# Three edits at the start of a fused attention and two-MLP kernel: coarse exponentials from PSUM, six products of zeros, and a new order of all steps

## The chip, the cores and the metric

The kernel runs on one core of one Trainium2 chip. The metric is the device time of one execution in microseconds. The core has five engines that this text calls TensorE (PE in the rows, PEld for its weight loads), VectorE (DVE), ScalarE (ACT), GpSimd (POOL) and SyncE (SP, which here issues all DMAs). Each works through its own queue in program order and waits on semaphores for the others.

## The reference

Attention of two kinds over q, k, v of 4 batches, 8 heads, 576 positions and 64 columns is added up, and two MLPs follow.

```python
q_d = q.reshape(B, H, Sd, 4, D).mean(axis=3)     # k_d, v_d likewise, Sd = 144
out_up = np.repeat(sm_attn(q_d, k_d, v_d), 4, axis=2)          # coarse
mask = np.abs(pos[:, None] - pos[None, :]) < 4
scores = np.where(mask, scale * q @ k.T, -1e9)                 # local
out = out_up + softmax(scores) @ v
x = out.transpose(0, 2, 1, 3).reshape(2304, 512)
h = x @ w_in;  x = (h * np.cos(h)) @ w_out                     # 512 -> 2048 -> 512
out = ((x @ w_a) * (x @ w_b)) @ w_out2                         # 512 -> 1536 -> 512
```

Both softmaxes subtract the maximum of a row, and divide by the sum plus 1e-9.

## The kernel before

The tokens are cut into eight units of 288 (two to a batch). A unit's attention is done in four head pairs `hp`, two of which form a `pr`. Every step of attention and of the first MLP is a key in the string `ORDER`, and the loop at lines 972 to 983 emits the steps in that order, so that each engine's queue is the order of the keys that fall to it. A key is a name, the unit and the pair, and after @ the engine (a ScalarE, d VectorE, p GpSimd) where there is a choice. The last third of the run, the second MLP, is emitted by loops and not by `ORDER`.

The steps of one unit:

- `sm` sums q and k in fours (line 373 on VectorE, three instructions at 375 to 377 on GpSimd); `lp` and `dp` are the local and the coarse scores on TensorE (398, 422). `vp` (344, unit 0 only) sums v in fours on TensorE.
- `lm` adds the mask and takes the maximum (405, 410), `lu` subtracts it (415), `le` is the exponential (442), `ln` and `lz` sum and divide (458 to 464).
- `dx` takes the coarse maximum (428). `da` writes maximum minus score into the tile `smd` (436 on ScalarE, 438 on VectorE), and `de` is its exponential with a scale of -1/128 and a row sum (449; each row sum shows as an extra ACTIVATION_READ_ACCUMULATOR). From unit 2 on (`DM` is 2) one `de` serves both pairs of a unit. `dn` and `dz` turn the sums into factors and apply them (476, 486).
- `lt`, `dt` transpose (493, 505), `lc`, `dc`, `vq`, `up` copy out of PSUM (290, 292), `at` multiplies with v (518 coarse, 525 local), `cb` adds the two parts (538), and `xh`, `xl` split the result into a rounded part and a rest (290 or 292, 560).

The first MLP: `w3.0` to `w3.4` convert the fourth block of weights in five stages (266, 269 on ScalarE, 271 on VectorE, a copy, a subtraction at 580). `h` (group g, part c) is three products of the first layer, `c` six stages of x cos x (656 to 668: ScalarE, VectorE, ScalarE, VectorE, a copy, a subtraction), `b` three products of the second layer. The stages c.4 and c.5, w.3 and w.4, and `xh` and `xl` may run on any engine that `ORDER` names. Exponential and sine need different tables of ScalarE, and a change of table is an ACT_TABLE_LOAD. Keys that begin with L are loads (`L0` the first ones: k and q of a pair, v for two pairs as `v` and `V`, weights as `w`), those with `p` prepare the second MLP's weights.

Scores of unit 0 go to several PSUM tags; from unit 1 on all of a unit's attention shares the one buffer of the tag `att`, so each use waits for the last reader of the one before. The tag `h` has two buffers.

Of the kernel before, what the change touches and what calls it, by code (L numbers as in the profile page):

```python
# [47 lines left out]
C = {'FS': 8, 'DM': 2, 'LAG': 3, 'NGS': 3, 'NGH': 4, 'NLAST': 9, 'CP': 24, 'SD0': 2, 'RA': 7, 'SA': 6, 'SD': 3, 'LG': 6, 'NXF': 3, 'LI': 2.5, 'LO': 2.5, 'L0': ['k0', 'k1', 'v0', 'V0', 'w0', 'k2', 'w1', 'k3', 'v1', 'V1', 'w2', 'w3', 'w4', 'w5', 'w6', 'w7']}  # L48
# [7 lines left out]
sm1.1@d Lc10 vq0.2@a ln0.1 lz0.1@d vq0.3@a Lc8 h0.0 w6.2@d h1.0 w9.1@a dz0.2@p dt0.1 dc0.1@a w3.0@a h1.1 Lq2.0 lt0.1 lc0.10@a lc0.11@a at0.1 w5.2@d  # L56
h2.0 h2.1 w6.3@d w10.1@a w9.2@d w3.1@a up0.1@d cb0.2 xh0.2@a cb0.3 w6.4@p w3.2@d h0.1 L0w7 sm1.0@d xh0.3@a xl0.3@d w8.1@a lp1.0 xl0.2@p h2.2 h1.2
w3.3@d h0.2 h0.3 w8.0@a w4.3@a w8.2@d w7.1@a lm1.0 c0.0@a w3.4@p Lc12 w4.4@p c0.1@d Lc15 Lk2.1 h1.3 c1.0@a c1.1@d Lc26 w7.0@a w7.2@d w7.3@d Lq1.2
w5.3@d h2.3 c2.0@a h3.0 h3.1 c0.2@a Lc13 h3.2 h3.3 c3.0@a dp1.0 c1.2@a dx1.0 w7.4@p Lq1.3 lu1.0@p c0.3@d da1.00@d c1.3@d lu1.1@d h5.0 h5.1 h5.2
da1.01@d sm1.2@d lp1.1 sm1.3@d w5.4@p c2.1@d Lk2.0 h4.0 Lc16 w12.0@a c0.4@d c1.4@d c1.5@p Lc27 w10.0@a w12.1@a w8.3@d Lc11 h4.1 lm1.1 h4.2 c0.5@p b0.1  # L60
w9.3@a h5.3 w10.2@d lu1.2@p le1.0 ln1.0 lz1.0@p de1.0 dn1.0 b0.0 Lc30 c2.2@a c3.1@d c2.3@d h4.3 dp1.1 dx1.1 da1.10@d w11.1@a c4.0@a Lc29 da1.11@d b1.0
lu1.3@p b0.3 b1.3 w8.4@d b1.1 dz1.0@p lt1.0 lc1.00@d lc1.01@d c3.2@a c3.3@d w9.4@d c2.4@a w13.0@a c2.5@p b2.0 b2.1 le1.1 dz1.1@p c3.4@d c3.5@p w15.1@a
dt1.0 ln1.1 dc1.0@a w10.3@a sm2.0@d b2.3 b0.2 w10.4@p b1.2 at1.0 b3.0 up1.0@d Lq2.1 c4.1@d w11.0@a cb1.1 c5.0@a b2.2 de1.1 b3.1 cb1.0 b3.3 dn1.1
lz1.1@p lt1.1 b3.2 c4.2@a Lw2.0 w11.2@d Lc18 lc1.11@a lc1.10@a Lc14 w11.3@a dz1.3@p sm2.1@d lp2.0 xh1.1@a c4.3@d c5.1@d lm2.0 vs2.0@p w15.0@a Lc24
xl1.1@d xh1.0@a w11.4@p h6.0 h6.1 Lc22 c4.4@a Lq2.2 dz1.2@p c5.2@a c5.3@d h6.2 Lc20 w14.1@a h6.3 c6.0@a w13.1@a lu2.1@p dt1.1 Lc19 dc1.1@d c5.4@a
c6.1@d w12.2@d c4.5@d h7.0 w14.0@a w12.3@a h7.1 at1.1 up1.1@a w14.2@d cb1.2 cb1.3 Lc25 c6.2@a c6.3@d h7.2 h7.3 c7.0@a xh1.2@a xh1.3@a xl1.0@p dp2.0
Lc21 w12.4@p b4.3 w13.2@d Lw2.1 Lk2.3 h8.0 w19.0@a b4.0 c7.1@d c7.2@a dx2.0 Lq2.3 c7.3@d w13.3@a h8.1 w20.1@a w20.0@a xl1.2@p h8.2 da2.00@d xl1.3@p
w15.2@d da2.01@d h9.0 h9.1 Lk2.2 h9.2 w27.0@a h9.3 vs2.1@p c6.4@a Lq3.0 lp2.1 c5.5@p h8.3 b4.1 w25.0@a w13.4@d b5.3 b5.1 sm2.3@d c6.5@p lm2.1 w14.3@a
w14.4@p Lc23 b4.2 b5.2 Lc17 b5.0 b6.0 lu2.0@p lu2.2@p c8.0@a c8.1@d w16.0@a Lc28 sm2.2@d c9.0@a c9.1@d b6.3 w24.0@a dp2.1 c8.2@a c8.3@d c7.4@d b6.1
lu2.3@p h10.0 w15.3@a w15.4@p dx2.1 da2.10@d h10.1 h10.2 c9.2@a le2.0 b6.2 Lv2 Lq3.2 da2.11@d h10.3 de2 c10.0@a c9.3@d c7.5@p b7.2 b7.0 ln2.0 Lw2.2  # L70
vs2.2@p h11.0 b7.1 le2.1 Lq3.1 lz2.0@p h11.1 c10.1@d c10.2@a dn2 h11.2 h11.3 c11.0@a c8.4@a c10.3@d b7.3 e7.0@d sm3.1@p e7.3@d lt2.0 dz2.0@p lc2.01@a
# [1199 lines left out]
```

## Time and profile before

| | us |
|---|---|
| median of three runs | 896.27 (894.94 to 896.31) |
| the profiled execution | 895.03 |
| its span from the first to the last instruction | 893.2 |
| TensorE busy | 872.7 (98%) |
| VectorE busy | 658.0 (74%) |
| ScalarE busy | 551.5 (62%) |
| GpSimd busy | 497.0 (56%) |

The profile's busy time of TensorE counts each product with its modelled end, so products overlap in it and a busy engine need not be at its peak. Idle time of an engine matters only where the engine that ends last waits for it. All times below are counted from the start of the span.

### The profile page before, as it was taken

To read this page: it belongs to the slowest core of one execution; us is meant where nothing else is said; L and a number is where in the kernel's file an instruction comes from. 1 tells how busy PE (TensorE), PEld (TensorE's weight loads), DVE (VectorE), ACT (ScalarE), POOL (GpSimd) and SP (SyncE) were. 2 spreads that over 40 slices of the span, in tenths; PEclk is the share of its full clock that TensorE was granted. 3 is DMA by queue.
4 is the path that set the end of the run, shared out by engine and by line. 5 is a ranking of instruction groups with operands and counts; after the bars stand their busy time and mean duration, and the time that the engine had idled before them with its cause. 6 is when DMAs were issued, how large, how long until landed. Compare 5 with 4: busy or idle time off the path is not lost.

```text
span 893.2 us, 17805 instructions
## 1 busy us (share of the span) xinstructions
PE 872.7 (98%) x6444; PEld 815.2 (91%) x6444; DVE 658.0 (74%) x1229; ACT 551.5 (62%) x1126; POOL 497.0 (56%) x656
## 2 busy tenths in 40 slices
...
GB/s 356 327 309 142 121 120 80 129 154 112 221 214 176 163 142 159 89 43 126 270 310 115 95 180 213 289 241 273 343 93 71 183 206 260 341 73 96 232 139 54
DMA packets 96935, 162.10 MB, mean 181 GB/s; under 512 B 6608, under 2 KB 64464, under 8 KB 96848
## 3 DMA queue, kind: packets, MB, share of 16 engines
...
## 4 chain that ended last, share of the span: by engine, by line
PE 93%; DMA 2%; DVE 2%; ACT 1%; POOL 1%; issue 1%; SPq 0%; POOLq 0%; ACTq 0%
PE z L587 15%; PE z L588 15%; PE z L589 15%; PE acc L587 8%; PE h L587 8%; PE acc L588 7%; PE acc L589 7%; PE h L588 7%; PE h L589 7%; PE att L398 1%; DMA raw<-in_w_in_dram 1%; PE att L422 1%; PE att L525 1%; DMA kq<-in_kq_dram 1%; PE att L493 1%; PE att L518 1%
## 5 line engine op out<-in xcount | busy, mean ns | idle before, releaser
L1006 POOL TENSOR_TENSOR sb<-w,sb 128x256 fp32r<-128x256 f32 x154 | 125.2, 825 | 121.0 <-ACT sb L1004 120.2
L1004 ACT ACTIVATE sb<-w 128x256 fp32r<-128x256 f32 x252 | 97.8, 415 | 51.6 <-PE z L589 43.4
L587 PE MATMUL h<-xbig,w 128*128 128x480 f32 (+3 forms) x352 | 128.1, 364 | 1.5 <-DVE gbig L662 1.5
L587 PE MATMUL acc<-tbig,w 128*128 128x480 f32 (+3 forms) x352 | 127.4, 362 | 0.5 <-DVE gbig L662 0.5
L588 PE MATMUL acc<-tbig,w 128*128 128x480 f32 (+3 forms) x352 | 124.5, 354 | 1.2 <-POOL tbig L668 1.2
L588 PE MATMUL h<-xbig,w 128*128 128x480 f32 (+3 forms) x352 | 124.2, 353 | 0.7 <-POOL xbig L560 0.7
L589 PE MATMUL acc<-tbig,w 128*128 128x480 f32 (+3 forms) x352 | 124.4, 353 | 0.1
L589 PE MATMUL h<-xbig,w 128*128 128x480 f32 (+3 forms) x352 | 124.0, 352 | 0.0
L668 POOL TENSOR_TENSOR tbig<-gbig,tbig 128x288 fp32r<-128x288 f32 (+3 forms) x47 | 51.7, 1102 | 96.5 <-ACT tbig L290 45.4
L656 ACT ACTIVATE gbig<-h,turn 128x480 int32<-128x480 f32 (+3 forms) x88 | 53.3, 607 | 69.7 <-PE h L589 63.9
L587 PE MATMUL z<-xbig,sb 128*128 128x384 f32 x288 | 96.2, 334 | 0.0
L589 PE MATMUL z<-xbig,sb 128*128 128x384 f32 x288 | 96.2, 334 | 0.0
L588 PE MATMUL z<-xbig,sb 128*128 128x384 f32 x288 | 96.2, 334 | 0.0
L658 DVE SCALAR_TENSOR_TENSOR gbig<-gbig,h 128x480 f32<-128x480 int32 (+3 forms) x88 | 51.3, 585 | 57.0 <-ACT gbig L656 56.5
L1006 DVE TENSOR_TENSOR sb<-w,sb 128x256 fp32r<-128x256 f32 x98 | 60.0, 614 | 21.8 <-ACT sb L1004 21.8
L587 PEld LDWEIGHTS h<-xbig,w 128*128 128x128 f32 x352 | 66.2, 188 | 10.5 <-DVE gbig L662 2.1
L587 PEld LDWEIGHTS acc<-tbig,w 128*128 128x128 f32 x352 | 66.2, 188 | 8.8 <-issue 1.5
L588 PEld LDWEIGHTS acc<-tbig,w 128*128 128x128 f32 x352 | 66.2, 188 | 7.8 <-POOL tbig L668 1.9
L588 PEld LDWEIGHTS h<-xbig,w 128*128 128x128 f32 x352 | 66.3, 188 | 6.8 <-POOL xbig L560 1.2
L589 PEld LDWEIGHTS acc<-tbig,w 128*128 128x128 f32 x352 | 66.1, 188 | 6.5 <-POOL w L580 0.3
L589 PEld LDWEIGHTS h<-xbig,w 128*128 128x128 f32 x352 | 66.2, 188 | 6.2
L660 ACT ACTIVATE gbig<-gbig,turn 128x480 f32<-128x480 f32 (+3 forms) x88 | 56.5, 644 | 22.9 <-DVE gbig L658 22.3
...
## 6 DMA issues: line engine op xcount, KB each, us to landing
...
```

Source lines behind the costliest of these rows:

```text
L398: pe.matmul(p[i][o, W * w:W * w + W], qt[u, 2 * pr + i][r, off:off + W], kt[u, 2 * pr + i][r, off:off + W], start=True, stop=True)
L422: pe.matmul(p[a][:QD, SD * i:SD * i + SD], qd[u, 2 * pr + i][r, :], kd[u // 2, 2 * pr + i][r, :], start=True, stop=True)
L493: pe.transpose(p[part][:, 128 * i:128 * i + 128], pt[u, pr][:, s], ident)
L587: i = pe.matmul(ps_out, lh, rh, start=start, stop=False, skip_group_check=more)
L588: pe.matmul(ps_out, lh, rl, start=False, stop=False, skip_group_check=more)
L589: pe.matmul(ps_out, ll, rh, start=False, stop=stop, skip_group_check=more)
L656: act.activation(out=gs[g].bitcast(I32), in_=hps[g], func=AF.Identity, scale=1.0 / (2.0 * math.pi), bias=turn[:, 0:1])
L658: dve.scalar_tensor_tensor(out=gs[g], in0=gs[g].bitcast(I32), scalar=-2.0 * math.pi, in1=hps[g], op0=ALU.mult, op1=ALU.add)
L660: act.activation(out=gs[g], in_=gs[g], func=AF.Sin, bias=turn[:, 1:2])
L668: eng.tensor_tensor(out=gl[g], in0=gs.pop(g), in1=gh[g].bitcast(F32), op=ALU.subtract)
L1004: act.activation(out=t[:, 0], in_=blk, func=AF.Copy)
L1006: (dve if nst[0] % (C["SD"] if G else C["SD0"]) == 0 else pool).tensor_tensor(out=t[:, 1], in0=blk, in1=t[:, 0].bitcast(F32), op=ALU.subtract)
```

## The change

- `down_exp` (units 0 and 1) reads the coarse scores from PSUM, and takes the maximum times -1/128 as a bias. That product is one more small instruction in `down_max`. The eight `down_neg` of these units are gone.
- `down_sums` is cut in two: `sm` sums q, a new step `sk` sums k for both halves of a batch.
- The array with the first q and k has q ahead of k now, and each of its four loads is two: `L0k` brings q and the first half of k, `L0K` the rest.
- Six new steps `fw` each multiply 128x128 zeros with 128x256 zeros into a PSUM tile that nobody reads; VectorE clears 384 columns of `gbig` for them. They stand ahead of the first scores.
- `ORDER` is new from end to end: other sequence and, for many steps, another engine. The keys are the same but for those above. Copies (`xh`, w.3, c.4) on GpSimd, of which the old order has none, occur 47 times.

The diff, with the first lines of both orders:

```diff
-C = {'FS': 8, ...
+C = {'NW': 6, 'FS': 8, ...
 ORDER = """
-L0k1 L0k0 lp0.0 sm0.0@p sm0.1@d dp0.0 L0w1 w1.0@a w1.1@a lm0.0 L0v0 L0k3 w1.2@d lu0.1@d L0V0 vp0.0 lu0.0@d dx0.0 L0w2 w1.3@d le0.0 ln0.0 lz0.0@d lt0.0
-da0.01@a da0.00@a de0.0 L0k2 L0w0 w2.1@a w2.0@a Lq1.1 L0w5 vq0.0@a vq0.1@a sm0.3@p lc0.00@a dn0.0 dz0.0@d dz0.1@p dt0.0 sm0.2@d dp0.1 lc0.01@a L0w4
-dc0.0@d at0.0 w0.1@a w1.4@p w2.2@d w2.3@a w2.4@p w0.0@a L0v1 dx0.1 w5.0@a L0w6 up0.0@d cb0.1 L0V1 xh0.1@a cb0.0 w5.1@a w0.2@d da0.11@a da0.10@d Lc9
-w0.3@d w0.4@p w4.1@a Lq1.0 xh0.0@d lp0.1 lm0.1 lu0.2@d de0.1 xl0.1@p w4.0@a vp0.1 w6.1@a lu0.3@d dn0.1 dz0.3@p le0.1 w6.0@a w9.0@a w4.2@d L0w3 xl0.0@p
...
+L0k0 L0K0 sm0.0@d sk0.0@p L0k1 sm0.1@d L0K1 sk0.1@d fw0 fw1 fw2 fw3 fw4 fw5 L0w1 w1.0@a lp0.0 lm0.0 lu0.1@p lu0.0@d L0v0 w1.1@a le0.0 dp0.0 dx0.0
+de0.0 L0V0 vp0.0 ln0.0 L0w2 w2.0@a dn0.0 w2.1@a dz0.0@a L0k2 L0K2 L0k3 L0K3 vq0.0@a lz0.0@d w1.2@d dz0.1@p w2.2@d dt0.0 w1.3@p dc0.0@a vq0.1@a w1.4@p
+L0w0 lt0.0 sk0.2@d sm0.2@d L0w5 lc0.00@a sk0.3@d L0v1 lc0.01@a sm0.3@d L0V1 w2.3@a w2.4@p w0.1@a at0.0 up0.0@d L0w4 dp0.1 cb0.0 cb0.1 dx0.1 w0.0@a
+w0.2@d lp0.1 lm0.1 w5.0@a de0.1 w5.1@a xh0.0@p lu0.2@d w4.1@a w4.0@a lu0.3@d le0.1 xh0.1@p w0.3@p vp0.1 w0.4@p Lq1.1 dn0.1 dz0.3@p xl0.0@p xl0.1@d
...
 """
@@ -299,10 +300,24 @@
                 sp.dma_start(out=t, in_=kT[b, hp, :, BASE[h]:BASE[h] + HALF])
                 kt[u + h, hp] = t
 
+    idle = []
+
+    def keep_warm():
+
+        if not idle:
+            idle.append(ps.tile([128, 256], F32, tag="acc0", name="idle"))
+        pe.matmul(idle[0], gbig[:, :128], gbig[:, 128:384], start=True, stop=True)
+
+    kq_rest = {}
+
     def first_kq(hp):
         t = wp.tile([128, S + HALF], F32, tag="w", name="kq", bufs=33)
-        sp.dma_start(out=t, in_=kq0[hp])
-        kt[0, hp], kt[1, hp], qt[0, hp] = t[:, :HALF], t[:, BASE[1]:S], t[:, S:]
+        sp.dma_start(out=t[:, :2 * HALF], in_=kq0[hp, :, :2 * HALF])
+        qt[0, hp], kt[0, hp], kt[1, hp] = t[:, :HALF], t[:, HALF:2 * HALF], t[:, HALF + BASE[1]:]
+        kq_rest[hp] = t
+
+    def first_k(hp):
+        sp.dma_start(out=kq_rest.pop(hp)[:, 2 * HALF:], in_=kq0[hp, :, 2 * HALF:])
 
     def load_q(u, hp):
         if u < NU:
@@ -376,14 +391,15 @@
             eng.tensor_tensor(out=out, in0=out, in1=v[:, :, 2], op=ALU.add)
             eng.tensor_tensor(out=out, in0=out, in1=v[:, :, 3], op=ALU.add)
 
+    def key_sums(eng, u, hp):
+        t = at.tile([128, SD], F32, tag="kd", name="kd", bufs=4)
+        for h in range(2):
+            o = NB * h - BASE[h]
+            sum4(eng, t[:, QD * h:QD * h + QD], kt[u + h, hp][:, o:o + NB])
+        kd[u // 2, hp] = t
+
     def down_sums(eng, u, hp):
-        b, half = divmod(u, 2)
-        if half == 0:
-            t = at.tile([128, SD], F32, tag="kd", name="kd", bufs=4)
-            for h in range(2):
-                o = NB * h - BASE[h]
-                sum4(eng, t[:, QD * h:QD * h + QD], kt[u + h, hp][:, o:o + NB])
-            kd[b, hp] = t
+        half = u % 2
         t = at.tile([128, QD], F32, tag="qd", name="qd", bufs=2)
         o = NB * half - BASE[half]
         sum4(eng, t, qt[u, hp][:, o:o + NB])
@@ -428,6 +444,8 @@
             dve.tensor_reduce(out=mxd[u, pr][:, s].rearrange("p a i -> p (a i)"),
                               in_=src.rearrange("p a (i k) -> p (a i) k", k=SD) if s.stop - s.start == 1 else
                               src.rearrange("p a (i k) -> p a i k", k=SD), axis=AX.X, op=ALU.max)
+        if u < C["DM"]:
+            dve.tensor_scalar(out=mxd[u, pr], in0=mxd[u, pr], scalar1=-1.0 / 128.0, scalar2=None, op0=ALU.mult)
 
     def down_neg(eng, u, pr, a):
         src, mx = dsp[u, pr][a][:QD, :2 * SD].rearrange("p (i c k) -> p i c k", c=NK, k=KD), mxd[u, pr][:, a]
@@ -445,8 +463,10 @@
         sdr[u, pr] = at.tile([QD, 4], F32, tag="sd", name="sd", bufs=2)
         for i in range(2):
             for a in range(2):
-                t, k = scores(pr, a, i), 2 * i + a
-                act.activation(out=t, in_=t, func=AF.Exp, scale=-1.0 / 128.0, accum_out=sdr[u, pr][:, k:k + 1])
+                k = 2 * i + a
+                src = dsp[u, pr][a][:QD, SD * i:SD * i + SD].rearrange("p (c k) -> p c k", k=KD)
+                act.activation(out=scores(pr, a, i), in_=src, func=AF.Exp, scale=1.0 / 128.0, bias=mxd[u, pr][:, a, i:i + 1],
+                               accum_out=sdr[u, pr][:, k:k + 1])
 
     def down_exps(u):
         t = smd[:QD].rearrange("p q a c m -> p (q a c) m")[:, :, :KD]
@@ -684,6 +704,7 @@
                            base=base, channel_multiplier=m)
     pool.memset(smd[:QD].rearrange("p q a c m -> p (q a c) m")[:, :, KD:64], 0.0)
     turn = const.tile([128, 3], F32, name="turn")
+    dve.memset(gbig[:, :384], 0.0)
     dve.memset(turn[:, 0:1], 0.25)
     dve.memset(turn[:, 1:2], math.pi / 2.0)
     down = turn[:, 2:3]
@@ -714,6 +735,8 @@
         for hp in range(HP):
             k = f"{u}.{hp}"
             put("sm" + k, down_sums, u, hp)
+            if u % 2 == 0:
+                put("sk" + k, key_sums, u, hp)
             put("lu" + k, local_sub, u, hp)
             put("dz" + k, down_norm, u, hp)
             put("cb" + k, combine, u, hp)
@@ -725,7 +748,7 @@
             put("lm" + k, local_max, u, pr)
             put("dp" + k, down_scores, u, pr)
             put("dx" + k, down_max, u, pr)
-            for a in range(2):
+            for a in range(2 if u >= C["DM"] else 0):
                 put(f"da{k}{a}", down_neg, u, pr, a)
             if u < C["DM"]:
                 put("de" + k, down_exp, u, pr)
@@ -761,7 +784,11 @@
 
     for what in C["L0"]:
         k = int(what[1:])
+        if what[0] == "k":
+            put(f"L0K{k}", first_k, k)
         put("L0" + what, *{"k": (first_kq, k), "v": (load_v, 0, (k,)), "V": (load_v, 1, (k,)), "w": (conv_load, k)}[what[0]])
+    for k in range(C["NW"]):
+        put(f"fw{k}", keep_warm)
     for pr in range(HP // 2):
         put(f"vp0.{pr}", pool_v, pr)
     for hp in range(HP):
@@ -1240,7 +1267,7 @@
     vds = vds.reshape(B, HP // 2, NK, 128, 2, 4, D)
     qT, kT = pairs(q), pairs(k)
     return {
-        "kq0": np.concatenate([kT[0], qT[0, :, :, :HALF]], axis=2), "qT": qT, "kT": kT, "vw": vw.reshape(NU, HP // 2, 128, NW, 2, D), "vds": vds,
+        "kq0": np.concatenate([qT[0, :, :, :HALF], kT[0]], axis=2), "qT": qT, "kT": kT, "vw": vw.reshape(NU, HP // 2, 128, NW, 2, D), "vds": vds,
         "w_in": cols(moe_w_in), "w_out": moe_w_out.reshape(NF, 128, DM),
         "w_a": blocks(moe2_w_a), "w_b": blocks(moe2_w_b), "w_out2": blocks_t(moe2_w_out),
     }
```

## Rows read from the trace of the kernel before

**Rows 1.** Busy time in five stretches, then granted clock, DMA share, GB/s
```profile
core 0: us, PE busy (x) PEld busy (x) DVE busy (x) ACT busy (x) POOL busy (x), PEclk, DMA share, GB/s
0.00:10.00 10.00, 2.38 (x48) 1.95 (x48) 4.00 (x11) 2.79 (x4) 7.17 (x25) 1.00 0.80 295
10.00:30.00 20.00, 15.38 (x306) 13.26 (x305) 18.57 (x45) 18.93 (x50) 13.25 (x18) 1.00 1.03 400
30.00:64.00 34.00, 29.31 (x423) 25.39 (x423) 32.18 (x76) 33.30 (x70) 25.88 (x27) 1.00 0.83 301
64.00:100.00 36.00, 35.99 (x489) 33.51 (x490) 34.05 (x76) 34.09 (x66) 30.61 (x44) 1.00 0.53 169
...
460.00:893.20 433.20, 429.63 (x2433) 424.34 (x2431) 320.89 (x571) 233.74 (x548) 240.99 (x266) 1.00 0.52 187
```

**Rows 2.** TensorE's waits: the longest of 10 to 64 us, all after 64
```profile
PE att L344 <- issue: 1.6, 1, 1.6
...
PE att L422 <- DVE xf L538: 0.4, 1, 0.4
```

**Rows 3.** ScalarE's waits between 10 and 64 us: total, times, longest
```profile
ACT smx L442 <- DVE smx L415: 1.7, 1, 1.7
ACT gbig L656 <- PE h L589: 0.2, 1, 0.2
```

**Rows 4.** Timeline: start, duration, engine, line, operation, out<-in, count, idle before
```profile
0.88 0.06 DVE L687 MEMSET turn<- 128x1 f32 x1 [0.88 <-PEq L1257]
...
5.33 1.34 PE L398 MATMUL att<-kq 64*64 64x64 f32 x40 [5.33 <-DMA kq<-in_kq_dram]
...
8.96 1.24 PE L422 MATMUL att<-kd,qd 64*72 64x144 f32 x8 [2.30 <-POOL qd L377]
...
10.75 0.74 ACT L442 ACTIVATE smx<-smx 128x640 f32<-128x640 f32 x1 [1.69 <-DVE smx L415]
...
17.07 0.61 PE L518 MATMUL att<-smd,vd 48*64 48x72 f32 x24
...
20.36 0.64 ACT L436 ACTIVATE smd<-att,mxd 72x144 f32<-72x144 f32 x2
...
22.22 2.82 PE L344 MATMUL att<-v,zsum 57*48 57x128 f32 x46 [1.56 <-issue]
...
25.20 0.79 POOL L560 TENSOR_TENSOR xbig<-xf,xbig 128x288 fp32r<-128x288 f32 x1
...
29.04 0.81 PE L525 MATMUL att<-smx,v 64*64 64x60 f32 x40 [0.17 <-ACT smx L290]
...
36.46 0.71 PE L422 MATMUL att<-kd,qd 64*72 64x144 f32 x8
...
63.96 0.71 PE L422 MATMUL att<-kd,qd 64*72 64x144 f32 x8 [0.37 <-DVE xf L538]
```

**Rows 5.** Line 344 alone in two stretches: TensorE, its loads, clock, DMA
```profile
10.10:12.66 2.56, 2.53 (x24) 2.46 (x26) 1.00 1.01 399
12.90:14.30 1.40, 1.39 (x26) 1.14 (x22) 1.00 1.04 417
```

**Rows 6.** Groups by form, 0 to 66 us: count, busy us, mean ns, idle before
```profile
L449 ACT ACTIVATE smd<-smd 72x144 f32<-72x144 f32 x16 | 4.9, 316 | 0.0
L660 ACT ACT_TABLE_LOAD x3 | 3.8, 1283 | 0.1
L436 ACT ACTIVATE smd<-att,mxd 72x144 f32<-72x144 f32 x6 | 1.8, 373 | 0.0
...
L438 DVE TENSOR_TENSOR smd<-mxd,att 72x288 f32<-72x288 f32 x5 | 2.1, 443 | 0.0
L476 DVE TENSOR_SCALAR sd<-sd 72x4 f32<-72x4 f32 x4 | 0.6, 156 | 0.0
```

**Rows 7.** The first loads: duration of an issue in ns (shortest, median, longest)
```profile
L304 SPq DMA_DIRECT2D kq<-in_kq_dram x4: 387/458/632, 0.8 to 4.2; - x4
```

**Rows 8.** GpSimd's groups by form, whole run: busy us, mean ns
```profile
L580 POOL TENSOR_TENSOR w<-raw,w 128x512 fp32r<-128x512 f32 x22 | 30.3, 1379 | 10.3 <-DVE w L292 5.5 <-ACT w L290 4.8
L683 POOL TENSOR_SCALAR_AFFINE_SELECT zsum<-zsum 128x544 f32<-128x544 f32 x2 | 1.3, 662 | 0.1
```

More of the change, by code (lines that the diff above doesn't have):

```diff
@@ L46 @@
 BASE = (0, 284)
[L48 removed]
+C = {'NW': 6, 'FS': 8, 'DM': 2, 'LAG': 3, 'NGS': 3, 'NGH': 4, 'NLAST': 9, 'CP': 24, 'SD0': 2, 'RA': 7, 'SA': 6, 'SD': 3, 'LG': 6, 'NXF': 3, 'LI': 2.5, 'LO': 2.5, 'L0': ['k0', 'k1', 'v0', 'V0', 'w0', 'k2', 'w1', 'k3', 'v1', 'V1', 'w2', 'w3', 'w4', 'w5', 'w6', 'w7']}
@@ L56 @@
[L56 to L71, printed above, removed]
@@ new lines @@
+de0.0 L0V0 vp0.0 ln0.0 L0w2 w2.0@a dn0.0 w2.1@a dz0.0@a L0k2 L0K2 L0k3 L0K3 vq0.0@a lz0.0@d w1.2@d dz0.1@p w2.2@d dt0.0 w1.3@p dc0.0@a vq0.1@a w1.4@p
+L0w0 lt0.0 sk0.2@d sm0.2@d L0w5 lc0.00@a sk0.3@d L0v1 lc0.01@a sm0.3@d L0V1 w2.3@a w2.4@p w0.1@a at0.0 up0.0@d L0w4 dp0.1 cb0.0 cb0.1 dx0.1 w0.0@a
+w0.2@d lp0.1 lm0.1 w5.0@a de0.1 w5.1@a xh0.0@p lu0.2@d w4.1@a w4.0@a lu0.3@d le0.1 xh0.1@p w0.3@p vp0.1 w0.4@p Lq1.1 dn0.1 dz0.3@p xl0.0@p xl0.1@d
+L0w6 w6.1@a h1.0 dz0.2@p w6.0@a vq0.2@a Lc9 w9.0@a vq0.3@a sm1.1@d w9.1@a h0.0 h0.1 ln0.1 lz0.1@d dt0.1 dc0.1@a lt0.1 lc0.10@a w6.2@d Lq1.0 sm1.0@d
```

190 lines of the change are left out of this document (103 added, 87 removed).

## The prediction

> **What bounds the kernel now.** I read the stretches first [rows 1], then what TensorE waits for [rows 2], what ScalarE waits for [rows 3], and then the start instruction by instruction [rows 4]. The stretches: TensorE is idle for 7.6 us of the first 10, 4.6 of the next 20 and 4.7 of the 34 up to 64 us, and from there it is busy without a break. The only wait above 0.15 us after 64 us is 0.4 us, at 63.96, and at the end 3.6 us go into the last evacuations and stores [rows 1, 2]. The change touches nothing behind 460 us, and it neither adds nor removes a product after the first scores. So the time can move by what the head (0 to 64 us, 16.9 us idle) gives, and by stalls that a new order may put where there are none.
>
> In the head ScalarE is the engine that decides: it is busy for 18.9 of 20 us and then for 33.3 of 34, and from 10 us on it waits for anything only once for long, 1.7 us before the first exponential [rows 1, 3]. VectorE is close behind (18.6 and 32.2), GpSimd is not (13.3 and 25.9). TensorE's idle time is thus the time that ScalarE and VectorE take for the weight conversions, the attention of two units and the first cosines. A head that ends earlier needs an earlier start of ScalarE's unbroken run at 10.75, or less work in it.
>
> **The change part by part.** *Coarse exponentials.* Units 0 and 1 lose eight `down_neg`: three on ScalarE, six instructions (373 ns each, but they overlap, 0.64 for two), and five on VectorE, 443 ns each [rows 4, 6]. Counted from start to start these are 6 x 0.26 = 1.6 us of ScalarE and 5 x 0.365 = 1.8 of VectorE. Added are four small `tensor_scalar` of 72x4 (row: 156 ns, 0.2 with its gap), 0.8 us of VectorE. The sixteen exponentials stay, each with its accumulator read. They now read PSUM and take a per-partition bias, like today's negation: 373 against 316 ns a piece [rows 6], so 16 x 0.057 = 0.9 us more. Net: ScalarE 0.7 us less, VectorE 1.0 us less.
>
> The Trainium skill ("ScalarE: Activation LUTs", section "What ACT_TABLE_LOAD costs") puts a pointer operand at about 93 ns, by which the sixteen would cost 1.5 us and ScalarE would win only 0.1. The rows have the smaller number.
>
> *PSUM.* In unit 1 the single `att` bank holds the coarse scores until ScalarE has done the exponentials, not until VectorE has subtracted. Behind it on TensorE stand `lp1.1` and, in its queue, `h4`. The order moves `dp1.0` ahead of `h3` to make room; below it costs 0.3 us.
>
> *Table loads.* Between exponentials and sines there are 21 changes of table in the old order and 21 in the new, 1.28 us each [rows 6]: nothing.
>
> *Loads.* Each first q/k load becomes two, q with the first half of k (299 KB) and the rest (145 KB). Today both pairs must land, 888 KB, which is at 5.33 [rows 4]. New, the first scores need three of the four parts, 743 KB; at 0.36 us per 145 KB, by the head's 400 GB/s [rows 1], they are there at about 4.95. Four more issues cost SyncE 0.46 us each [rows 7], hidden by a DMA share of 1.0. `v1` and `V1`, which hold TensorE up for 1.6 us at 22.2 today (nothing else is open there), move ahead of `w4`, `w6` and a q load: that wait should go, but what is late next is the split of x (25.99), so alone it is worth nothing.
>
> *Six products of zeros.* Six times 256 columns in fp32, which the trace records as two passes, as for `pool_v`. A pass of 128 columns took 0.21 us for two side by side up to 12.66 (24 in 2.53 us) and half of that from 12.9 (26 in 1.39) [rows 5]: the engine ran at the lower of its two levels up to there, although the clock column says 1.00. So 12 x 0.43 = 5.1 us at the lower level. They start when VectorE has cleared `gbig`, about 1.45 (an estimate: it sets its first constants at 0.88 [rows 4], and 384 columns come on top), and end at 6.6, or at 5.7 if the clock rises while they run. That is later than the data (4.95): the first scores start at 5.7 to 6.6 and not at 5.33, but at the upper level they take 0.6 to 0.9 instead of 1.34 [rows 4, 5]. I take their end as 7.4 (6.6 to 7.95; today 6.67).
>
> *The order.* `dp0.0` waits till 8.96 for GpSimd's nine sums [rows 4]; with six it is free at 7.3, and `w1.2` no longer stands ahead of the subtraction. Chain with today's durations: `lm0.0` 7.5 to 9.2, `lu0.0` 9.7, `dx0.0` with negation 10.6, `le0.0` 10.0 to 10.65, `de0.0` 12.1; `le0.0` began at 10.75 today. Then ScalarE does `w2`, `dz0.0`, the copies out, and `at0.0` starts at 16.35 (17.07 today). Now a new wait: `dx0.1` stands on VectorE behind `up0.0` and both `cb`, so it ends at 19.85, while ScalarE is ready for `de0.1` at 18.7: 1.1 us idle, and behind it are queued `w5.1`, `w4` and `le0.1`. After that I get x of chunk 0 split at 24.9 (25.99), the second `attend` over at 29.35 (29.85), `h0` to `h3` and `dp1.0` done at 36.65 (37.1), `dp2.0` at 62.9 (63.96) [rows 4]. ScalarE and VectorE have per product about what they have today. So the head ends 0.45 to 1.05 us earlier; I take 0.9.
>
> *New kind of work.* GpSimd gets 47 plain copies in the whole order, which it does not do today. Bounds for 512 columns: its select over 544 columns took 0.66, its subtraction over 512 1.38 [rows 8]. I take 0.65, as a copy has one input like the select; at 1.38 `c1.5` comes 1.7 us later, of which 1.0 reaches TensorE. Below the lower bound there is nothing to win, since GpSimd has slack. In the saturated part ScalarE's and VectorE's loads fall slightly, GpSimd's 30.6 of 36 us between 64 and 100 grows by about 3 [rows 1]: no stall, unless a copy sits in a chain.
>
> **Sum.** The profiled execution took 895.03 us, 893.2 of it span. Less 0.9: 894.1. The three runs shown lie at 894.94, 896.27 and 896.31; the mean of all four is 895.6. Less 0.9 that is **894.7**, which I give. About 0.2% (1.8 us) is what a measurement can tell from no change.
>
> **The rivals.** *A, a larger gain.* The clock rises early in the six products (scores over at 6.6, 0.8 us better), and the new wait before `de0.1` does not appear since VectorE's work there is shorter than I add up (1.1 us). Both kept to the end: 0.9 + 1.9 = 2.8 less, 892.8. For: ScalarE never waits today [rows 3]; against: VectorE is nearly as full. Chance 0.25.
>
> *B, the six products do not do what they say.* The clock is still low when the first scores run: they end at 7.95, 1.3 later than today, the coarse maxima follow, and ScalarE has lost its lead at `de0.1`: 0.5 less to 0.5 more, 895.6. Chance 0.12.
>
> *C, the clock falls back.* After `pool_v` (over at about 11) TensorE idles some 3 us till `dt0.0`; the longest idle since the rise is 1.6 us today, without a loss of pace [rows 2, 4]. At the lower level `dt0.0`, `lt0.0` and `at0.0` take 2.1 us more, of which 1.1 reaches the split: 895.8. The Trainium skill ("TensorE: Matmul & The Clock Gate", section "Why this matters for your kernels") warns of just such gaps between bursts, which speaks against the six products; no run here shows it yet. Chance 0.08.
>
> *D, slower: GpSimd's copies.* If 512 columns cost over about 1.8 us, the nine instructions from `w7.3` to `c1.5` (36.5 to 44.4 in my chain, three of them copies) push `b0` and `b1` out by over 2 us, and the same comes back in each chain `c.4`, `c.5` on GpSimd. At 2.5 us: three times 1.85, less 1.2 of slack, 4.4 late on a lead of 0.9, of which TensorE makes up 1 with `b` products that are ready: 898.1. Against: no row shows GpSimd slower than 2.7 ns an element [rows 8]. Chance 0.12.
>
> **How the numbers follow.** Forecast 0.43 (893.7 to 895.4 by the end of the first scores alone), A 0.25, B 0.12, C 0.08, D 0.12. The range reaches into A and D, and takes in the 0.7 us by which runs scatter: 892.2 to 898.0. Faster by over 0.2% (below 893.8) gets most of A and a tenth of the forecast, 0.28; slower (above 897.4) D and little else, 0.14; the rest 0.58.
>
> **What would show it.** Right: the first scores after 5.7, at 0.9 us or less for 40; `le0.0` near 10.0; ScalarE idle before `de0.1` for about a microsecond; the unbroken run of TensorE from about 63 instead of 64; the same 21 table loads. Wrong: waits of TensorE after 64 us, GpSimd copies above 1.4 us, 40 scores at 1.34 us again, or a head whose idle time shrinks by 3 us or more.

## The result, and the profile after

| | us |
|---|---|
| kernel before, median of four runs | 895.99 (894.94 to 896.31) |
| changed kernel, median of four runs | 904.61 (902.97 to 905.85) |
| ratio | 1.0093 [1.0081, 1.0105] |
| profiled execution, its span | 904.53, 902.5 |

Slower by 8.6 us, where I forecast 894.7. Behind 460 us nothing differs: the first product of the second MLP starts 9.4 us later than before (505.27 instead of 495.83), and the last ends 9.4 us later. Executions in which the clock was low throughout (w18_early once took 1076.76 us at a mean granted clock of 0.752) are left out of the medians and ratios below. The stretches of [rows 1], now for the changed kernel, with one more (us, busy time and count of TensorE, its weight loads, VectorE, ScalarE, GpSimd, then granted clock, DMA share, GB/s):

```profile
0.00:10.00 10.00, 7.98 (x82) 6.10 (x84) 4.39 (x13) 2.80 (x4) 6.36 (x22) 1.00 0.79 263
10.00:30.00 20.00, 14.15 (x227) 12.07 (x221) 16.58 (x41) 16.62 (x42) 10.87 (x12) 0.83 0.97 375
30.00:64.00 34.00, 28.29 (x409) 24.13 (x409) 31.18 (x67) 31.74 (x67) 23.24 (x27) 1.00 0.81 296
64.00:100.00 36.00, 34.28 (x439) 31.58 (x440) 33.16 (x70) 32.37 (x62) 33.19 (x46) 1.00 0.49 164
100.00:140.00 40.00, 37.78 (x458) 35.80 (x457) 37.89 (x69) 34.54 (x66) 30.91 (x40) 0.96 0.34 99
```

Between 10 and 64 us ScalarE has 3.9 us more idle time than before, and behind 64, where TensorE never paused, 3.9 us are missing from it up to 140. Twice the clock is at the lower level (1.2 GHz) for a while, which [rows 1] never show (up to 10 us the column says 1.00 here too, although the zeros ran at half pace). TensorE's longest waits (total, times, longest), against [rows 2]:

```profile
PE h L607 <- DVE gbig L682: 4.0, 4, 1.7
PE att L525 <- POOL smd L506: 3.9, 1, 3.9
...
PE h L608 <- POOL xbig L580: 1.3, 1, 1.3
```

The timeline shows where they come from (most lines stand 15 to 20 higher than in the kernel before: `dz` is L506, `xl` L580, `at` L538 and L545, the cosine stage c.3 L682; w.2 is L272):

```profile
1.39 5.45 PE L309 MATMUL idle<-gbig 128*128 128x256 f32 x12 [1.39 <-DVE turn L712]
6.76 0.81 PE L414 MATMUL att<-kq 64*64 64x64 f32 x40
...
13.04 0.79 DVE L484 TENSOR_TENSOR smx<-smx,sl 128x640 f32<-128x640 f32 x1
13.75 1.28 DVE L272 SCALAR_TENSOR_TENSOR raw<-raw 128x512 uint32<-128x512 uint32 x2
...
13.27 2.29 POOL L506 TENSOR_TENSOR smd<-smd,sd 72x288 f32<-72x288 f32 x1 [2.76 <-DVE sd L497]
...
15.62 0.59 PE L525 MATMUL att<-ident,smd 72*112 72x72 f32 x6 [3.94 <-POOL smd L506]
16.90 1.38 PE L538 MATMUL att<-smd,vd 48*64 48x72 f32 x21 [0.15 <-ACT smd L291]
...
18.08 1.38 PE L545 MATMUL att<-smx,v 64*64 64x60 f32 x39
...
16.32 0.53 ACT L291 ACTIVATE smd<-att 112x432 f32<-112x432 f32 x1 [1.44 <-PE att L525]
...
21.77 0.38 ACT L468 ACTIVATE smd<-att,mxd 72x144 f32<-72x144 f32 x1 [1.29 <-DVE mxd L448]
...
36.31 0.71 PE L438 MATMUL att<-kd,qd 64*72 64x144 f32 x8
...
68.10 0.71 PE L438 MATMUL att<-kd,qd 64*72 64x144 f32 x8 [0.36 <-DVE xf L558]
...
131.29 0.72 POOL L431 TENSOR_TENSOR smx<-smx,mx 128x320 f32<-128x320 f32 x1
131.98 2.59 POOL L600 TENSOR_TENSOR w<-raw,w 128x512 fp32r<-128x512 f32 x2
134.51 0.81 POOL L688 TENSOR_TENSOR tbig<-gbig,tbig 128x288 fp32r<-128x288 f32 x1
...
131.61 4.25 DVE L272 SCALAR_TENSOR_TENSOR raw<-raw 128x512 uint32<-128x512 uint32 x1
...
136.28 0.56 PE L607 MATMUL h<-xbig,w 128*128 128x288 f32 x1 [1.75 <-DVE gbig L682]
136.64 0.44 PE L608 MATMUL h<-xbig,w 128*128 128x288 f32 x1
```

Three places. *The head:* `dz0.1` took 2.29 us on GpSimd (its shortest run elsewhere in the kernel took 0.66) while VectorE ran `lz0.0` and two w.2; TensorE waited 3.94 us for it, the clock fell, and the attention of unit 0 ran at half pace (granted clock 0.50) until 23.6: 39 products of L545 took 1.38 us, where 40 took 0.81 in [rows 4]. *Unit 1:* `dp2.0` started at 68.10 instead of 63.96, although `dp1.0` had started at the same time as before, 36.31 [rows 4]. Not all of these 4.1 us arise there: the four steps `h3`, ahead of `dp1.0` in the old order, stand behind it in the new one (1.7 us of TensorE, from 36.95), so that much is a debt of the head. TensorE's idle time from `dp1.0` to `dp2.0` grew from 4.6 to 6.5 us. *131 us:* w18.2 on VectorE stood for 4.25 us instead of 0.69 and ended half a microsecond behind GpSimd's three instructions; TensorE waited 1.75 us for the step behind it, and its products then took 0.44 instead of 0.29 us until 139.7.

### The profile page after: what moved, and what is told of

Read it like the earlier page. It is cut to its first block, busy times and chain, and to the rows that moved or that the text cites. A ratio compares the mean times of both kernels' runs of the same rounds, so it can differ in the third digit from the quotient of the medians.

```text
span 902.5 us, 17803 instructions
## 1 busy us (share of the span) xinstructions
PE 881.4 (98%) x6456; PEld 821.4 (91%) x6456; DVE 663.6 (74%) x1209; ACT 539.9 (60%) x1102; POOL 521.1 (58%) x679
## 4 chain that ended last, share of the span: by engine, by line
PE 87%; DVE 5%; ACT 3%; DMA 2%; POOL 2%; issue 1%; SPq 0%; DVEq 0%; ACTq 0%; POOLq 0%
PE z L609 15%; PE z L608 15%; PE z L607 15%; PE acc L607 7%; PE h L607 7%; PE h L608 6%; PE acc L609 6%; PE acc L608 6%; PE h L609 6%; DMA raw<-in_w_in_dram 1%; PE att L545 1%; PE att L538 1%; DVE raw L272 1%; PE att L513 1%; PE att L438 1%
## 5 line engine op out<-in xcount | busy, mean ns | idle before, releaser
L607 PE MATMUL h<-xbig,w 128*128 128x480 f32 (+3 forms) x352 | 128.8, 366 | 4.0 <-DVE gbig L682 4.0
L607 PE MATMUL acc<-tbig,w 128*128 128x480 f32 (+3 forms) x352 | 127.6, 363 | 1.1 <-DVE gbig L682 1.1
L607 PE MATMUL z<-xbig,sb 128*128 128x384 f32 x288 | 96.2, 334 | 0.0
L607 PEld LDWEIGHTS h<-xbig,w 128*128 128x128 f32 x352 | 66.7, 189 | 14.1 <-DVE gbig L682 4.2
L688 POOL TENSOR_TENSOR tbig<-gbig,tbig 128x480 fp32r<-128x480 f32 (+3 forms) x51 | 55.8, 1099 | 40.2 <-DVE tbig L293 29.7
L607 PEld LDWEIGHTS acc<-tbig,w 128*128 128x128 f32 x352 | 66.4, 189 | 9.3 <-DVE gbig L682 1.6
```

Of the source, the lines that this page charges most:

```text
L607: i = pe.matmul(ps_out, lh, rh, start=start, stop=False, skip_group_check=more)
L688: eng.tensor_tensor(out=gl[g], in0=gs.pop(g), in1=gh[g].bitcast(F32), op=ALU.subtract)
```

## The experiments

All times beside runs of the kernel before on the same chip; the ratio is to those.

| run | us | ratio to the kernel before |
|---|---|---|
| old_loads | 896.40 | 1.0004 [0.9993, 1.0016] |
| old_zeros | 896.52 | 1.0008 [0.9999, 1.0017] |
| old_unit0 | 895.90 | 0.9995 [0.9983, 1.0007] |
| old_order | 902.19 | 1.0069 [1.0046, 1.0091] |
| old_order_zeros | 904.65 | 1.0091 [1.0070, 1.0113] |
| new_head | 898.55 | 1.0022 [1.0012, 1.0032] |
| new_head_no_zeros | 898.48 | 1.0021 [1.0011, 1.0031] |
| new_then_old | 900.54 | 1.0047 [1.0032, 1.0062] |
| old1_then_new | 900.94 | 1.0059 [1.0044, 1.0075] |
| old_then_new | 909.90 | 1.0145 [1.0130, 1.0160] |
| c21_first | 904.36 | 1.0096 [1.0081, 1.0111] |
| w18_early | 902.27 | 1.0073 [1.0056, 1.0090] |
| old1_then_new_w18 | 897.70 | 1.0025 [1.0015, 1.0035] |
| unit1_through_sbuf | 904.79 | 1.0108 [1.0091, 1.0125] |
| more_zeros | 904.02 | 1.0091 [1.0076, 1.0107] |
| dz_on_vector | 903.00 | 1.0084 [1.0069, 1.0099] |

### The edits one by one, in the old order

`PX` is the number of units whose exponentials read PSUM; the others have their `da` back.

```diff
 old_loads, old_zeros (PX = 0), old_unit0 (PX = 1), old_order, old_order_zeros (PX = 2)
-        if u < C["DM"]:
+        if u < C["PX"]:
...
-ORDER of the changed kernel
+ORDER of the kernel before, with sk beside sm and L0K behind L0k
+PX > 0: lt0.0 behind de0.0, de0.1 in place of the last da0.1
+PX = 2: de1.0, de1.1 in place of the last da; c3.2 c3.3 behind le1.1
+old_zeros, old_order_zeros: fw0 to fw5 ahead of lp0.0
```

> The changed kernel's code (coarse exponentials of units 0 and 1 straight from PSUM, first loads in two) in the order of the kernel before, without the six products of zeros. Each exponential stands where the last negation stood, because the next user of the PSUM buffer may only come behind it; one sine of unit 1 moves behind the exponential that it would have split. Theory 1 (the new order loses the time, in three places: the head, the one PSUM buffer of unit 1, 131 to 140 us): close to the kernel before, 894.5 to 897.5, the rest of it lost in unit 1, where the buffer is held until ScalarE is done. Theory 2 (the order is innocent, the exponentials from PSUM cost the time): 901 or more. Theory 3 (the order alone, the edits are worth what I forecast): 894.5 to 895.5.

> The same, with the six products of zeros ahead of the first scores. Theory 1: the zeros end at about 6.8 us instead of the 5.3 at which data is there, the scores then run at the upper clock (0.8 instead of 1.34 us), so the scores end within 0.9 us of the run without zeros, and the total is within 1 us of it. If the clock falls again in the idle time of TensorE behind the sums of v, as it did in the changed kernel, the total is 1 to 3 us above the run without zeros.

> The changed kernel's code in the order of the kernel before, with none of the coarse exponentials from PSUM and no zeros: all that is left of the change is the first loads in two parts with q ahead of k. Theory A (the loads cost nothing): 895 to 896.5, first scores within 0.3 us of 5.33. Theory B (four more loads push the loads of v back, for which TensorE waited at 22.2 us already): 897 to 898.

> The same with the six products of zeros ahead of the first scores. Theory A (with the upper clock from 6.8 us the sums of v are over early, TensorE then idles in longer pieces, the clock falls and the half pace comes into the attention of unit 0): a stretch at the lower clock between 10 and 40 us, 1 to 3 us above the run with the loads alone. Theory B (the head hides it): no more than 0.7 us above it. Theory C (the zeros do what they are for): 0.5 us or more below it.

> The old order without zeros; unit 0 takes its coarse exponentials straight from PSUM, unit 1 goes through SBUF as in the kernel before. It splits the 5.8 us that both units together cost in the old order. Theory A (the one PSUM buffer of unit 1 is the costly part): from dp1.0 to dp2.0 27 to 28 us as in the kernel before instead of 35.7, and the total at 896 to 899, what is left being unit 0. Theory B (unit 0 and the loads cost it): 901 or more.

Loads, zeros and unit 0 each measure as nothing, although the first scores of old_loads began at 6.00 us, 0.7 later than before. On top of old_order the zeros stand 2.5 us worse, but the two intervals overlap. The cost of the edits, 6.3 us between old_unit0 and old_order, comes with unit 1, whose attention has one PSUM buffer. ScalarE in old_order:

```profile
50.49 0.50 ACT L676 ACTIVATE gbig<-h,turn 128x288 int32<-128x288 f32 x1 [0.64 <-PE h L609]
52.20 1.28 ACT L468 ACT_TABLE_LOAD   x1 [1.21 <-DVE mxd L448]
53.49 0.38 ACT L468 ACTIVATE smd<-att,mxd 72x144 f32<-72x144 f32 x1
```

TensorE's longest waits between 36 and 76 us in the same run (total, times, longest):

```profile
PE h L607 <- DVE gbig L682: 3.3, 2, 1.8
PE att L513 <- issue: 2.3, 1, 2.3
PE att L414 <- ACT smd L468: 0.8, 1, 0.8
```

And unit 1 as a row like those of [rows 1], first in old_order, then in old_unit0:

```profile
36.00:76.00 40.00, 32.06 (x378) 28.66 (x377) 31.04 (x69) 32.18 (x68) 24.09 (x26) 0.83 0.78 278
```

```profile
36.00:66.00 30.00, 25.35 (x366) 21.82 (x364) 28.24 (x68) 29.60 (x65) 22.88 (x25) 1.00 0.89 324
```

ScalarE was free at 51.0, but the exponential's table came only once VectorE's maximum was there, at 52.2; only then followed the load (1.28) and the exponentials (to 54.9), and `lt1.0` (L513) started at 55.14, after 2.3 us of waiting. 3.1 us wait directly for the exponentials (L513 and L414), and between 36 and 76 us the granted clock was 0.83 on average, where old_unit0 has 1.00. From `dp1.0` to `dp2.0` both kernels have the same 344 products of TensorE, in 35.7 us here and 27.5 in old_unit0: 3.3 of the 8.2 us are idle time (7.9 instead of 4.6), and 4.9 are the same products at the slower pace (27.8 us busy instead of 22.9). So in this run, 905.79, the slowest of the five, the fall of the clock cost more than the waiting. The five roughly follow their mean granted clocks, from 900.05 us at 0.996 to 905.79 at 0.988. What the two moved cosine steps cost, and whether their waits (L607) brought the clock down, was not separated.

### The new order in stretches

Each takes one order up to a step and the steps that are left in the other order. `old1` is the order of old_unit0.

```diff
-ORDER of the changed kernel
+new_then_old:  new up to dp2.0, then that of old_order
+old_then_new:  that of old_order up to dp2.0, then new
+old1_then_new: old1 up to dp2.0, then new
+new_head:      new up to dp1.0 (PX = 1), then old1
+new_head_no_zeros: the same without fw0 to fw5
```

> The new order up to the coarse scores of unit 2 (68 us), and from there the steps that are left in the old order. Theory 1: keeps the loss of the head and of unit 1 (the coarse scores of unit 2 start 4.1 us late) and loses nothing at 131 us: 899 to 900.5. Theory that the loss is spread over the whole order: 897 or less. Theory that most of it comes from the head: 903 or more.

> The old order (as in the run of the changed code in the old order, without zeros) up to the coarse scores of unit 2, and from there the steps that are left in the new order. Theory 1: no loss in the head, and 3.5 us at about 131 us if VectorE is held by GpSimd there again: 898 to 901; without that hold 895 to 898. Theory that the head makes all the loss: 894.5 to 896.

> The old order with only unit 0 from PSUM and without zeros (which by itself took the time of the kernel before) up to the coarse scores of unit 2, then the new order. If the late part of the new order costs by itself what the trace of the changed kernel shows there (1.0 us from dp2.0 to dp4.0, 3.8 from dp4.0 to at4.0): 900 to 901.5. If that was only the echo of an earlier lateness: 896 to 897.5.

> The new order with the six products of zeros up to dp1.0 (36 us), unit 1 through SBUF, and from there the steps that are left in the old order. The head by itself: if it costs what TensorE's progress at dp1.0 says (0.9 to 1.5 us), 897 to 897.5, and the 2.7 us of unit 1 belong to the new order behind dp1.0; if the head leaves work undone that comes back in unit 1, 899 or more; if the head is a gain as I forecast, 895.3.

> The run new_head without the six products of zeros. Theory A (the zeros lift the clock early, TensorE then idles 3.9 us and falls back into the attention of unit 0): without them the sums of v end later, the gap is shorter and no stretch at the lower clock follows behind at0.0; 896 to 897.5 instead of 898.6. Theory B (the order of the head costs it, not the clock): 898 to 899.5.

By the ratios: the head alone 2.0 us, head and unit 1 together 4.2, what follows `dp2.0` alone 5.3. The last two add up to 9.5, and the changed kernel has 8.3; with intervals of 1.1 to 1.4 us each way these agree, so nothing here asks for more than the sum of the parts. old_then_new stacks the unit 1 of old_order and the late part (the sum is 11.5, the run has 13.0). The zeros change nothing in the new head either: without them the first four scores started at 3.62 us, but the other 36 had to wait for data until 5.99 and took 1.33, over at 7.32. In new_head the clock rose within the zeros (4.65 us instead of 5.45), and the 40 scores were over at 6.78; but the coarse scores then waited 0.6 us for GpSimd's sums and started at 7.36, as they did without zeros, at 7.32. So half of rival A came true there and won nothing. The clock was at 0.79 between 10 and 30 us without the zeros (0.80 with them), although the wait for `dz0.1` was 2.6 instead of 3.6 us: Theory A of that run falls.

### w18.2

```diff
 c21_first
-c21.2@a w18.2@d h22.1 c21.3@d b18.1
+c21.2@a h22.1 c21.3@d w18.2@d b18.1
 w18_early, old1_then_new_w18
-c20.2@a c20.3@d w27.3@a ... c21.2@a w18.2@d h22.1 ... w16.4@p
+c20.2@a w18.2@d c20.3@d w27.3@a ... c21.2@a h22.1 ... w16.4@d
```

> The changed kernel with two neighbours of VectorE's queue exchanged: c21.3, for which TensorE waits at 136.28 us, ahead of w18.2, which took 4.25 us there instead of 0.69. Theory A (VectorE's instruction with two SBUF inputs stood still while GpSimd ran five instructions without a gap, and TensorE's wait of 1.75 us then cost the upper clock up to 139.7): w18.2 still takes over 2 us, but nobody waits for it, TensorE's wait and the half pace behind it are gone, 3.5 us less: 901. Theory B (VectorE and GpSimd are late there anyway): the wait moves to another step within 10 us, 904 to 905.

> The changed kernel with w18.2 some 3 us earlier on VectorE, ahead of c20.3, where GpSimd idles, and with w16.4 on VectorE instead of GpSimd, which shortens GpSimd's run without a gap from 130.7 to 135.3 by 1.3 us. Theory A (a two-input instruction of VectorE stands still until GpSimd's run has a gap): w18.2 takes 0.7 us instead of 4.25, no other instruction there over 2 us, no wait of TensorE at 136, and nothing that comes back: 900.5 to 901.5. Theory B (VectorE has too much work there, whatever stands still): 903 to 905.

> The same with w18.2 earlier and w16.4 on VectorE, as in the run w18_early. If VectorE's standstill is the whole of the loss from dp4.0 to at4.0: 3.5 us less than old1_then_new, 896.5 to 898. If only the part that w18_early won as a whole: 2 us less.

The last two runs also move w16.4 from GpSimd to VectorE. The timeline's row of w18.2 in c21_first, and TensorE's longest wait behind it:

```profile
132.50 3.21 DVE L272 SCALAR_TENSOR_TENSOR raw<-raw 128x512 uint32<-128x512 uint32 x1
```

```profile
PE att L438 <- DVE xf L558: 2.0, 1, 2.0
```

The same two of old1_then_new (c.3 is L686 there):

```profile
127.45 4.24 DVE L272 SCALAR_TENSOR_TENSOR raw<-raw 128x512 uint32<-128x512 uint32 x1
```

```profile
PE h L611 <- DVE gbig L686: 1.9, 2, 1.7
```

And old1_then_new_w18, where TensorE's longest wait behind 64 us is 0.5:

```profile
126.10 0.68 DVE L272 SCALAR_TENSOR_TENSOR raw<-raw 128x512 uint32<-128x512 uint32 x1
```

With another neighbour (c21_first) the instruction still stood, until GpSimd's three had ended, and TensorE's wait only moved to `dp4.1`, with half pace behind it: no gain. Three microseconds earlier, counted from the w.2 ahead of it, it took 0.68, nothing came back, and 3.1 us were won (5.3 to 2.2 by the ratios; 1.8 in w18_early). So that standstill, with the half pace behind it, is most of the late part, as far as the second move (w16.4) did not add to the gain, which was not run alone; the 2.2 that remain are spread over steps that I did not single out.

### Unit 1 and the head of the new order

```diff
 unit1_through_sbuf (PX = 1)
-dx1.0 ... dx1.1
+dx1.0 da1.00@d da1.01@d ... dx1.1 da1.10@d da1.11@d
 more_zeros
-de0.0 L0V0 vp0.0 ln0.0
+de0.0 L0V0 vp0.0 fw6 fw7 fw8 fw9 fw10 fw11 fw12 fw13 ln0.0
 dz_on_vector
-lz0.0@d w1.2@d dz0.1@p w2.2@d
+lz0.0@d dz0.1@d w1.2@d w2.2@d
```

> The changed kernel, but unit 1 as in the kernel before: VectorE writes maximum minus score to SBUF (four da, right behind dx), and the exponentials read SBUF. Only unit 0 keeps the exponentials straight from PSUM. Theory A (in unit 1 the one PSUM buffer of the attention was held until ScalarE had done the exponentials, 5.7 us from the end of dp1.0 to lp1.1 and 5.8 from dp1.1 to lt1.0, against 2.9 and 2.6 in the kernel before): each hold shrinks by 2 to 3 us, dp2.0 starts 2 to 3 us earlier than 68.1, and the total falls by 2 to 3: 901.5 to 902.5. Theory B (the sequence of the other steps is what makes unit 1 late): dp2.0 stays within 0.7 us of 68.1 and the total at 904 to 905.5.

> The changed kernel with eight more products of zeros behind the sums of v (vp0.0), 3.4 us at the upper clock, in the 3.94 us in which TensorE idles for dz0.1. Theory A (the clock fell because of that idle time, and cost 3.3 us of TensorE from 16.9 to 23.6): no stretch at the lower clock up to 30 us, at0.0 over at 18.1 instead of 19.4, the second split of x over 1 to 2 us earlier, total 902.5 to 903.5. Theory B (the half pace was hidden, since ScalarE and VectorE end last there): clock up, but the total within 0.7 us of 904.6.

> The changed kernel with dz0.1, the second scaling of the coarse exponentials, on VectorE behind lz0.0 (0.5 us) instead of on GpSimd, where it took 2.29 us beside two-input instructions of VectorE. Theory A (that collision is what made the gap of 3.94 us): dt0.0 starts at about 14.6 instead of 15.6, and if the shorter gap of some 2.9 us keeps the clock up, at0.0 is over at 16.3 instead of 19.4, total 902 to 903; if the clock falls all the same, 903.5. Theory B: dt0.0 waits for something else, no change, 904 to 905.

None of the three differs from the changed kernel by more than the intervals. In unit1_through_sbuf `dp1.0` to `dp2.0` took 31.2 us instead of 31.8 (27.5 before): in the new order the held buffer costs little, and its waits there (0.4 us before `lp1.1`, 0.8 before `lt1.0`) say the same. Apart from these two, TensorE's waits between `dp1.0` and `dp2.0` (0.2 to 1.4 us, for VectorE, ScalarE and GpSimd) add up to some 5.3 us in the changed kernel, against 4.6 for all of them in the kernel before: unit 1 is late by the moved `h3`, by the two waits and by a little of everything, and which change of place causes the rest stays open. In the head the wait moved. TensorE's waits between 10 and 36 us in dz_on_vector:

```profile
PE h L608 <- POOL xbig L580: 2.4, 1, 2.4
PE att L525 <- DVE smd L506: 2.4, 1, 2.4
```

The stretches behind each, as rows like those of [rows 1]:

```profile
16.00:20.00 4.00, 4.00 (x114) 3.46 (x112) 3.45 (x12) 2.91 (x6) 3.10 (x4) 0.57 1.04 401
...
26.00:31.00 5.00, 4.77 (x82) 4.13 (x81) 3.24 (x7) 4.53 (x10) 1.69 (x1) 0.55 0.55 214
```

`dt0.0` came 1.6 us earlier, but after the shorter wait of 2.4 us the clock fell all the same (0.57 from 16 to 20); TensorE then stood another 2.4 us in front of the split of x and ran at the lower level again from 26 to 31. With more zeros the first gap was filled (clock 1.00 from 12 to 23), the second was 2.7 us, and the clock fell there (0.54 from 26 to 29). In both runs the other engines kept TensorE waiting at the split of x, so shortening or filling the first gap only moved idle time and slow stretches.

### What the two engines do to each other

Two small programs time one instruction of VectorE beside a run on GpSimd, and the other way round: port_probe with plain operands, port_probe2 with those of w.2, w.4, `lu`, c.5, `lz` and `dz`.

```diff
+for n in 0, 1, 2, 3, 5:
+    n x pool.tensor_tensor(out=run, in0=lead, in1=oth, op=ALU.subtract)      # 128x512
+    dve.scalar_tensor_tensor(out=one, in0=foll, scalar=0.5, in1=oth, ...)    # or a copy, a reduce, ...
```

> Leaves the whole computation out; its output is zeros. It measures one instruction of VectorE beside a run of 0 to 5 subtractions of 128x512 on GpSimd (about 1.3 us each, no gap between them), and the other way round one instruction of GpSimd beside a run on VectorE. Theory A (who holds the way to SBUF keeps it until its run has a gap): VectorE's instruction with two SBUF inputs, 0.7 us alone, ends 0.7 us behind the end of GpSimd's run, so about 1.7 us beside one subtraction, 3 beside two, 4.3 beside three, 7 beside five; an instruction with one input or with one input in PSUM keeps its own time; GpSimd's scaling of 72x288, 0.67 alone, waits in the same way for a run of VectorE. Theory B (one instruction is waited for, then they take turns): at most 2.0 us whatever the length of the run. Theory C (no such hold): 0.7 us throughout.

> Leaves the whole computation out; its output is zeros. The same measurement with the operands of the kernel: the merge of a weight block (w.2, unsigned integers, every second word, written back in place) on VectorE beside runs of GpSimd (plain subtractions, the subtraction of a weight block, and the sequence of lu, w.4, w.4, c.5 that stood beside w18.2, with an instruction that reads PSUM or a sum ahead of w.2), and GpSimd's scaling dz beside lz and two merges on VectorE. Theory A (the form of the operands decides: the merge in place, or the subtraction of a weight block, leaves no turn): w.2 beside three subtractions of a weight block takes 4 us or more, the plain forms 1.6. Theory B (the instruction ahead of it in the queue decides, which ends while the other engine runs): over 3 us only in the cases with an instruction ahead of w.2, whatever its operands, plain ones too. Theory C (turns in every case): 1.3 to 2.0 us everywhere, and the standstill in the kernel stays open.

port_probe, VectorE and GpSimd: the merge alone, beside one and beside five subtractions; `tensor_scalar` of 72x4 alone and beside one; a sum beside three; the run of five:

```profile
7.53 0.69 DVE L71 SCALAR_TENSOR_TENSOR one_a<-foll,oth 128x512 f32<-128x512 f32 x1 [0.94 <-ACT foll L97]
9.39 1.61 DVE L71 SCALAR_TENSOR_TENSOR one_a<-foll,oth 128x512 f32<-128x512 f32 x1 [1.17 <-ACT foll L97]
...
21.31 1.61 DVE L71 SCALAR_TENSOR_TENSOR one_a<-foll,oth 128x512 f32<-128x512 f32 x1 [3.51 <-ACT foll L97]
...
34.00 0.17 DVE L77 TENSOR_SCALAR one_c<-foll 72x4 f32<-72x4 f32 x1 [3.51 <-ACT foll L97]
35.34 1.09 DVE L77 TENSOR_SCALAR one_c<-foll 72x4 f32<-72x4 f32 x1 [1.17 <-ACT foll L97]
...
50.45 0.45 DVE L80 TENSOR_REDUCE one_e<-foll 128x72 f32<-128x288 f32 x1 [1.17 <-ACT foll L97]
...
21.11 6.59 POOL L65 TENSOR_TENSOR run_a<-lead,oth 128x512 f32<-128x512 f32 x5 [0.98 <-ACT lead L96]
```

They take turns: 1.61 us beside runs of one, two, three and five, so Theory A falls in this form. port_probe2 gives turns as well, w.2 behind a stage that reads PSUM and beside `lu`, w.4, w.4, c.5 among its cases:

```profile
30.29 1.80 DVE L79 SCALAR_TENSOR_TENSOR foll<-foll 128x512 uint32<-128x512 uint32 x1
```

So waiting for one instruction of the other engine is shown, and that w18.2 stood until GpSimd's three were done is shown by its rows in six kernels (4.24 to 4.26 us, 3.21 where it began 0.9 later) and by what moving it won; why it got no turn is not.

## Why the prediction was wrong

*What bounds the kernel.* Right that the time moves by the head and by new stalls only. Wrong in effect was "no stall" for the saturated part: I counted loads of engines there and looked at no collisions. That step alone missed 5.3 us, and most of it (3.1 us, with w16.4) came back when w18.2 was moved, which VectorE could not finish while GpSimd worked (4.25 us instead of 0.69).

*The coarse exponentials.* 0.36 to 0.38 us each, as taken (0.373). (The 0.057 that I put on PSUM and bias is no price of the bias: in the trace of before, with source and target in SBUF, 128x288 took 0.44 as a copy and 0.53 as a sine with a bias, so the source in PSUM seems to give some of it back.) The small product took 0.17 in unit 0 (0.156 taken) but 0.72 and 0.76 in unit 1, each time until a `lu` on GpSimd ended:

```profile
38.96 0.73 POOL L431 TENSOR_TENSOR smx<-smx,mx 128x320 f32<-128x320 f32 x1
...
38.99 0.72 DVE L448 TENSOR_SCALAR mxd<-mxd 72x4 f32<-72x4 f32 x1
```

*PSUM.* "Below it costs 0.3 us" is the worst term: in the old order the direct waits for the held buffer were 3.1 us, and with the half pace that came with unit 1 the edit cost 6.3; in the new order its direct waits are 1.2, and unit 1 lost some 2 us by the ratios. I priced the exponentials' own time and left out that the table load stands behind the same wait, and what the waits do to the clock.

*Loads.* The last of the first q and k were there at 6.04 instead of 4.95 (VectorE's second sum starts then); in total they are worth nothing either way.

*Zeros.* 5.45 us from 1.39 (5.1 from 1.45 taken), the scores 0.81 us as forecast, their end 7.57 instead of 7.4. Rival B is refuted in its mechanism (the scores ran at the upper level), and "worth nothing" holds in both orders, where the edits of unit 1 are left out.

*The order in the head.* `le0.0` at 10.54 (10.0), the new wait of ScalarE before `de0.1` 1.29 (1.1), `at0.0` at 16.90 (16.35): near. The split of x of chunk 0 ended at 27.05 instead of 24.9: `dz0.1` held for 1.6 us (ScalarE, whose unbroken run was to carry the head, waited 1.44 for the transposes behind it), and rival C's fall of the clock, which I gave 0.08 and expected after some 3 us of idle time; it came after 3.94. By its stretch it cost more than the 2.1 us of TensorE that I took (6.7 us at the lower level are 3.3 lost), but its share in the total is not shown: shortening or filling the gap won nothing, with slow stretches left elsewhere, and in the old order such stretches were free (old_loads was at 0.79 from 24 to 32 us, and took the time of the kernel before). The head as a whole lost 2.0 where I had 0.9 of gain; which of its steps lose them stays open.

*Rival D.* Its size is refuted: a copy of 512 columns took 0.68 on GpSimd (0.65 taken):

```profile
L293 POOL CAST w<-raw 128x512 fp32r<-128x512 f32 x7 | 4.7, 676 | 5.3 <-DVE raw L272 5.2
```

What I should have weighed was not how long GpSimd takes for new work but whom it holds while it works. The Trainium skill ("SBUF — State Buffer", section "Who interferes with whom") says that an instruction of VectorE with two inputs in SBUF contends with one of GpSimd that reads SBUF, as does one in a two-port mode, and that whichever issues first keeps the shared pair of ports for its whole instruction while the other blocks. The probe's rows agree (0.69 to 1.61 beside one of 1.26); the 4.25 us of w18.2 are more than the rule gives.
